# Where TensorE's operands start in SBUF: moving five tile pairs of a spectral MLP kernel to other offsets within 128 bytes

## The chip, the cores and the metric

The kernel runs on one core of a Trainium2 chip. The metric is the device time of one execution in microseconds. The reported time is the median of three runs. One further execution was recorded by the hardware profiler; every duration below comes from that one.

## The reference

The input `x` has 8 sequences of 3008 steps with 256 features. The reference takes a real FFT along the sequence, applies a complex 256 by 256 linear layer with bias to every frequency, soft-thresholds real and imaginary parts at 0.01, transforms back, and sends the 24064 resulting tokens through a two-layer MLP (256 to 2048 to 256) with a leaky ReLU:

```
X = rfft(x, axis=1);  Xr, Xi = X.real, X.imag
Yr = Xr @ w_r - Xi @ w_i + b_r
Yi = Xr @ w_i + Xi @ w_r + b_i
Yr, Yi = sign(Y) * max(abs(Y) - 0.01, 0)      # each of the two
y = irfft(Yr + 1j*Yi, n=3008, axis=1)          # 24064 tokens x 256
h = y @ moe_w_in;  g = max(0.01*h, h)
out = g @ moe_w_out
```

The MLP's weights arrive as float64 and are converted on the chip.

## The kernel before, in words

**Number format.** Nearly every product is made of float32 numbers that are split into a high and a low part in the format fp32r. A product is then three matmuls: high by high, high by low, low by high (`products`, L80, and `block`, L94, both helpers that record every product under one line). Each matmul needs a load of its 128 stationary columns, then streams 256 or 512 moving columns.

**Stages.** The FFT of length 3008 = 47 x 64 is done as small dense transforms. `fwd` (per sequence) folds and transforms over the 47: stationary `fa0`/`fa1`, moving `xz`, in PSUM tag psf. `mid` transforms over the 64 (`stage_b`, L358, plain float32, stationary `u`, moving `fb`), multiplies by the linear layer (`proj`: stationary `eh`, the transformed data; moving the 256-column weights `wr`, `wn`, `wd`), thresholds, and transforms back over the 64 (`stage_g`: stationary `gb`, moving `zh`, 512 columns). `inverse` (L495, plain float32) transforms back over the 47. `forms` makes the moving operands `yh`, `yl` of the MLP.

**The MLP.** Tokens go in 47 chunks of 512. The first layer (`moe_a`, `moe_b`, L94) uses seven products of 256 moving columns in place of eight: stationary `win_hi`/`win_lo`, moving `yh`/`yl`. Chunk 0 alone is done by `direct` with 512 moving columns. ScalarE and VectorE apply the leaky ReLU and split the result into `gh` and `gl` (`halves`, L573 and L575). The second layer (`moe_o`, L622) has stationary `wout_hi`/`wout_lo` and moving `gh`/`gl`, 512 columns.

**Order.** `moe` emits, for each of 8 steps of each chunk, the 21 matmuls of `moe_a`/`moe_b` and then 12 of `moe_o`, in the order in which they stand in the program. The work of `fwd`, `mid` and `inverse` for later sequences is fed between them by `Stream.to`, so that TensorE meets runs of one kind of matmul that are now and then broken by runs of another kind. A planner inside the tile framework sets the order of the rest from its own cost estimates; nothing in them depends on an operand's address.

**Places.** A tile is one stretch of bytes in each partition. The framework puts tiles one behind the other in steps of 32 bytes. `pair` allots constants with 32 floats to spare and starts them `skip` floats (4 bytes each) in. The list of tile addresses of the built program gives these starts, modulo 128 bytes:

| product | line | moving columns | matmuls | stationary starts at | moving starts at |
|---|---|---|---|---|---|
| first MLP layer, chunks 1 to 46 | L94 | 256 | 7728 | `win` 0 | `yh`,`yl` 64 |
| first MLP layer, chunk 0 | L94 | 512 | 96 | `win` 0 | `yh`,`yl` 64 |
| second MLP layer | L622 | 512 | 4512 | `wout` 64 | `gh`,`gl` 64 |
| linear layer (`proj`) | L80 | 256 | 1512 | `eh` 64 | `wr`,`wn`,`wd` 96 |
| `stage_g` | L80 | 512 | 252 | `gb` 64 | `zh` 64 |
| `stage_a` | L80 | 512 or 256 | 216 and 36 | `fa0`,`fa1` 64 | `xz` 64 |

Within one tile all slices that a matmul reads lie a multiple of 512 bytes apart, so every matmul of a row has the row's starts. The plain float32 matmuls (L358, L495 and those of the first sequences) are not in the table.

Of the kernel before, what the change touches and what calls it, by code (L numbers as in the profile page):

```python
# [9 lines left out]
F32R = mybir.dt.float32r  # L10
# [10 lines left out]
P = 128  # L21
PA = NK1 * NG
# [8 lines left out]
def spectral_mlp_kernel(  # L31
# [18 lines left out]
    D = w_r.shape[0]  # L50
    DF = w_in.shape[1]
    NF = DF // P
    NH = D // P
    NPAIR = NK1 // 2
    NQ = NF // 2
    NT, HT = 512, 256
# [9 lines left out]
    sb = ctx.enter_context(tc.tile_pool(name="sb", bufs=2))  # L66
# [4 lines left out]
    def bank(tag, bufs):  # L71
        return ps.tile([P, 512], F32, name=tag, tag=tag, bufs=bufs)
# [29 lines left out]
    def pair(name, shape, skip, spare=0):  # L102

        n = 1
        for s in shape[1:]:
            n *= s
        room = -(-n // 32) * 32 + 32
        tiles = [
            const.tile([shape[0], room + k], F32R, name=f"{name}_{p}")[:, skip:skip + n]
            for p, k in (("hi", 0), ("lo", spare))  # L110
        ]
        if len(shape) == 4:
            tiles = [t.rearrange("p (a b c) -> p a b c", a=shape[1], b=shape[2]) for t in tiles]
        elif len(shape) == 3:
            tiles = [t.rearrange("p (a b) -> p a b", a=shape[1]) for t in tiles]
        consts[name] = tuple(tiles)
        return consts[name]

    def load_plain(name, src, shape):
        consts[name] = const.tile(shape, F32, name=name)  # L120
        sync.dma_start(consts[name], src)

    def split_consts():
        for name in ("wr", "wd", "wn", "gb", "fa0", "fa1"):
            w = consts[name + "32"][0]
            hi, lo = pair(name, list(w.shape), 16 if name[0] == "w" else 8, 32 if name == "gb" else 0)
            act.copy(hi, w)
            dve.tensor_sub(lo, w, hi.bitcast(F32))

# [60 lines left out]
    def load_wout():  # L190

        n = CS // D
        ov = w_out.bitcast(U32).rearrange("(a p) f -> p a f", p=P)
        raws = []

        def load(early):
            k = len(raws)
            tag, bufs = ("gl", 2) if early else (("e", 1), ("z", 1))[k % 2]
            raw = sb.tile([P, CS, 2], U32, name="raw", tag=tag, bufs=bufs)
            with tc.issue_after(reads[13 if early else -1].ins):  # L200
                sync.dma_start(raw.rearrange("p (a f) w -> p a (f w)", a=n), ov[:, k * n:(k + 1) * n, :])
            raws.append(raw)

        for k in range(2):
            load(True)
        yield 1
        consts["wout"] = tuple(
            sb.tile([P, NF, D], F32R, name=f"wout_{p}", tag=f"wout_{p}", bufs=1) for p in ("hi", "lo"))
        for c in range(NF // n):
            a = sb.tile([P, CS], F32, name="cva", tag="zf", bufs=1)  # L210
            q = sb.tile([P, CS], F32, name="cvq", tag="u", bufs=3)
            float64_parts(raws[c], a, q)
            dh, dl = (w[:, c * n:(c + 1) * n, :] for w in consts["wout"])
            a, q = (t.rearrange("p (a f) -> p a f", a=n) for t in (a, q))
            act.copy(dh, a)
            dve.tensor_sub(a, a, dh.bitcast(F32))
            converted.append(dve.tensor_add(dl, a, q))
            yield 1
            while c >= 1 and len(raws) < min(c + 3, NF // n):
                load(False)  # L220
# [10 lines left out]
    def fwd(b):  # L231
        ud = dram.tile([2, NK1, NG * NS, D], F32, name="u_dram", tag="u_dram", bufs=NPRE + 1)
        u_dram[b] = ud
        uv = ud.rearrange("c k (g s) d -> c (k g) (s d)", g=NG)
        x_t, s_t = {}, {}

        def load(c):
            cols = slice(2 * c * D, min(2 * c + 2, NS) * D)
            n = cols.stop - cols.start
            if b < NPRE:  # L240
                tag, bufs = (XT, XT1)[b][c]
                x2 = sb.tile([PA, 2, 2 * D], F32, name="xin", tag=tag, bufs=bufs)
                x_t[c] = [x2[:, h, :n] for h in range(2)]
            else:
                x_t[c] = [
                    sb.tile([PA, 2 * D], F32, name=f"xin{h}", tag="uv"[h], bufs=3 - h)[:, :n] for h in range(2)
                ]
            for h, t in enumerate(x_t[c]):
                if b == 0:
                    (act if h else sync).dma_start(t, x[b, h, :, cols])  # L250
                else:
                    with tc.issue_after(reads[-1].ins):
                        sync.dma_start(t, x[b, h, :, cols])

        def fold(c):
            xa, xb = x_t[c]
            n = xa.shape[1]
            eng = dve
            xs = sb.tile([PA, 2 * D], F32, name="xs", tag="zf", bufs=1)[:, :n] if b else xs3[:, c % 3, :n]
            eng.tensor_add(xs, xa, xb)  # L260
            eng.tensor_sub(xa, xa, xb)
            s_t[c] = [(xs,), (xa,)] if b < NPRE else [xs, xa]

        def split(c, h):
            t = s_t[c][h]
            n = t.shape[1]
            z = sb.tile([PA, 2, 2 * D], F32R, name="xz", tag="ez"[h], bufs=1)
            xh, xl = z[:, 0, :n], z[:, 1, :n]
            dve.tensor_copy(xh, t)
            dve.tensor_sub(xl, t, xh.bitcast(F32))  # L270
            s_t[c][h] = (xh, xl)

        def stage_a(c, h):
            t = x_t[c][h]
            n = t.shape[1]
            pa = (bank("psf", 2) if b else bank("psh", 4))[:PA, :n]
            products(pa, [(consts[f"fa{h}"] if b else consts[f"fa{h}32"], s_t[c][h])])
            t = x_t[c][1 - h]
            cp = act.copy(t, pa)
            if b == 0:  # L280
                turned[:] = [cp]
            st = (act if b else sync).dma_start(uv[h, :, 2 * c * D:2 * c * D + n], t)
            if b == 0:
                written.append(st)

        def stage_a1(c):

            n = x_t[c][0].shape[1]
            pas = [(bank("psf", 2) if c in (4, 5) else bank("psh", 4))[:PA, :n] for _ in range(2)]
            for h in range(2):  # L290
                with tc.issue_after(turning[NPAIR - 2].ins):
                    products(pas[h], [
                        (consts[f"fa{h}32"], (x_t[c][0],)), (consts[f"fa{2 * h}32"], (x_t[c][1],))])
            for h in range(2):
                act.copy(x_t[c][h], pas[h])
                sync.dma_start(uv[h, :, 2 * c * D:2 * c * D + n], x_t[c][h])

        if b == 1:
            for c in range(NX):
                load(c)  # L300
                yield 0
            for c in (0, 1, 2, 3, 6, 4, 5):
                stage_a1(c)
                yield 6 * x_t[c][0].shape[1]
            return

        ahead = 2 if b >= NPRE else NX
        for c in range(ahead):
            load(c)
        yield 4 * CS if b >= NPRE else 0  # L310
        fold(0)
        if b >= NPRE:
            split(0, 0)
        yield 0
        for c in range(NX):
            for h in range(2):
                if h == 0 and c + ahead < NX:
                    load(c + ahead)
                if h == 0 and c + 1 < NX:
                    fold(c + 1)  # L320
                stage_a(c, h)
                if b >= NPRE and (c + h < NX):
                    split(c + h, 1 - h)
                yield 3 * x_t[c][h].shape[1]


    def mid(b):
# [21 lines left out]
        def stage_b(j):  # L349
# [4 lines left out]
            for i in range(2):  # L354
                k = 2 * j + i
# [4 lines left out]
            if b == 0:  # L360
# [2 lines left out]
                dve.tensor_add(ef[:, :, 2, :], ef[:, :, 0, :], ef[:, :, 1, :])  # L363
                e_t[j] = (ef,)
                return
            e2 = sb.tile([P, 2, NH, 3, P], F32R, name="eh", tag="e", bufs=1)
            eh, el = e2[:, 0], e2[:, 1]
            xi = sb.tile([P, NH, P], F32, name="xi", tag="xi", bufs=1)
            act.copy(xi, pv[:, :, 1, :])
# [7 lines left out]
        def proj(j):  # L377

            e = e_t.pop(j)
# [21 lines left out]
            t = sb.tile([P, 2, D], F32, name="t", tag="t" if b else "v", bufs=1 if b else 2)  # L401
# [12 lines left out]
            if b == 0:  # L414
                z_t[j] = (zf,)
                yield 6 * D
                return
            z = sb.tile([P, 2, 2, D], F32R, name="zh", tag="z", bufs=1)
            zh, zl = z[:, 0], z[:, 1]
            act.copy(zh, zf)  # L420
            dve.tensor_sub(zl, zf, zh.bitcast(F32))
# [147 lines left out]
        halves(ci, q, g)  # L569

    def halves(ci, q, g):
        gh = sb.tile([P, 4, HT], F32R, name="gh", tag="gh")
        cp = act.copy(gh, g)  # L573
        gl = sb.tile([P, 4, HT], F32R, name="gl", tag="gl")
        parted[:] = [cp, dve.tensor_sub(gl, g, gh.bitcast(F32))]  # L575
        g_t[ci, q] = (gh, gl)

# [154 lines left out]
    with tc.issue_after(reads[3].ins):  # L732
        load_plain("ga", ga, [PA, 2, P])
# [152 lines left out]
```

## Time and profile before

| what | value |
|---|---|
| median of 3 runs | 2558.36 us (2555.57 to 2559.72) |
| profiled execution, its own time | 2558.46 us |
| its span, first to last instruction | 2556.7 us |
| mean granted TensorE clock | 0.995 |
| TensorE matmuls busy | 2515.7 us (98%), 16204 records |
| TensorE weight loads busy | 2259.0 us (88%) |
| VectorE busy | 1881.0 us (74%) |
| ScalarE busy | 1673.5 us (65%) |
| GpSimd busy | 119.3 us (5%) |

Busy time of TensorE is a sum of durations that overlap: a matmul of 256 columns is shown as some 280 ns long while the next starts some 115 ns after it. What a matmul costs in a stream is therefore the distance from its start to the next start, which the timeline gives to 10 ns; over a run of matmuls the distance is exact enough to divide. The duration of one, given to the nanosecond, moves with that distance. A plain float32 matmul stands in the trace as two records.

### The profile page before, as it was taken

How to read it: one execution, taken by the hardware profiler on the slowest of the kernel's cores; microseconds unless marked ns; L12 is line 12 of the kernel's file. 1: busy time of each engine (PE TensorE's matmuls, PEld its weight loads, DVE VectorE, ACT ScalarE, POOL GpSimd, SP SyncE). 2: the span in 40 equal slices, each digit the busy share in tenths (PEclk: the TensorE clock that was granted, in tenths of full speed). 3: DMA queues.
4: the chain of work that ended last, by engine and by line, in shares of the span. 5: the costliest groups of instructions: out<-in, count | busy, mean ns of one | idle time of the engine just before them, and what ended most of it. 6: DMA issues, size and time to landing. Idle time of an engine off the chain costs nothing.

```text
span 2556.7 us, 42449 instructions
## 1 busy us (share of the span) xinstructions
PE 2515.7 (98%) x16204; PEld 2259.0 (88%) x16204; DVE 1881.0 (74%) x3460; ACT 1673.5 (65%) x3151; POOL 119.3 (5%) x96
## 2 busy tenths in 40 slices
PE   6999999999999999999999999999999999999999
PEld 4689888999899998999989999899998998999998
DVE  7787777777877778777787777876768777666675
ACT  4776666677666776667756676566665676656564
POOL 0001000000000000000000000000000000000000
PEclk8999999999999999999999999999999999999999
DMA  8631133111321113211142111411114111101000
GB/s 262 184 93 49 44 88 91 42 46 49 102 70 42 50 41 109 61 51 50 38 113 58 50 45 42 113 57 50 46 38 123 55 51 44 46 17 33 9 17 17
DMA packets 119904, 165.12 MB, mean 65 GB/s; under 512 B 13597, under 2 KB 69909, under 8 KB 119701
## 3 DMA queue, kind: packets, MB, share of 16 engines
q1 hardware_dynamic: 79112, 115.54, 14.9%
q10 hardware_dynamic: 40589, 46.87, 7.1%
q8 instruction: 128, 2.10, 0.3%
q14 instruction: 75, 0.61, 0.1%
HBM read 86.60 MB, written 75.76 MB: 64 GB/s over the span
## 4 chain that ended last, share of the span: by engine, by line
PE 90%; DMA 4%; DVE 3%; ACT 2%; issue 1%; SPq 1%; ACTq 0%; DVEq 0%
PE pso L622 38%; PE psh L94 34%; PE psf L80 11%; PE psf L495 3%; PE psf L358 3%; DMA xin<-x_dram 1%; PE psh L80 1%; DMA u<-u_dram 1%; DVE gl L575 1%; DMA u_dram<-xin 1%; DVE xz L270 0%; DMA v_dram<-v 0%; DVE gf L606 0%; ACT zf L413 0%; DMA vin<-v_dram 0%
## 5 line engine op out<-in xcount | busy, mean ns | idle before, releaser
L94 PE MATMUL psh<-yh,win_hi 128*128 128x256 f32 (+1 forms) x2608 | 737.2, 284 | 2.4 <-DVE gf L606 2.4
L94 PE MATMUL psh<-yl,win_hi 128*128 128x256 f32 (+1 forms) x2608 | 727.0, 279 | 0.0
L94 PE MATMUL psh<-yh,win_lo 128*128 128x256 f32 (+1 forms) x2608 | 726.5, 280 | 0.0
L575 DVE TENSOR_TENSOR gl<-gf,gh 128x1024 fp32r<-128x1024 f32 x376 | 461.1, 1226 | 309.7 <-ACT gh L573 300.5
L622 PE MATMUL pso<-gh,wout_hi 128*128 128x512 f32 x1504 | 592.3, 394 | 1.1 <-ACT gh L573 1.1
L622 PE MATMUL pso<-gh,wout_lo 128*128 128x512 f32 x1504 | 590.4, 393 | 0.0
L622 PE MATMUL pso<-gl,wout_hi 128*128 128x512 f32 x1504 | 588.7, 391 | 1.1 <-DVE gl L575 1.1
L94 PEld LDWEIGHTS psh<-yh,win_hi 128*128 128x128 f32 x2608 | 489.3, 188 | 19.9 <-DVE gf L606 4.9
L94 PEld LDWEIGHTS psh<-yl,win_hi 128*128 128x128 f32 x2608 | 490.5, 188 | 15.6 <-issue 0.5
L94 PEld LDWEIGHTS psh<-yh,win_lo 128*128 128x128 f32 x2608 | 489.1, 188 | 2.0
L573 ACT CAST gh<-gf 128x1024 fp32r<-128x1024 f32 x376 | 395.4, 1052 | 45.1 <-PE pso L622 35.3
L609 ACT ACTIVATE gf<-gf 128x768 f32<-128x768 f32 x368 | 311.8, 847 | 158.7 <-DVE gf L606 147.6
L622 PEld LDWEIGHTS pso<-gl,wout_hi 128*128 128x128 f32 x1504 | 282.6, 188 | 61.9 <-DVE gl L575 3.0
L622 PEld LDWEIGHTS pso<-gh,wout_hi 128*128 128x128 f32 x1504 | 282.7, 188 | 48.4 <-ACT gh L573 1.9
L622 PEld LDWEIGHTS pso<-gh,wout_lo 128*128 128x128 f32 x1504 | 282.6, 188 | 45.4 <-issue 0.2
L608 ACT ACTIVATE gf<-psh 128x256 f32<-128x256 f32 x368 | 141.6, 385 | 229.8 <-PE psh L94 223.4
L606 DVE TENSOR_TENSOR gf<-psh,u 128x512 f32<-128x512 f32 x368 | 252.7, 687 | 27.7 <-PE psh L94 25.3
L590 ACT COPY p<-psh 128x256 f32<-128x256 f32 x368 | 136.7, 371 | 153.3 <-PE psh L94 144.7
L395 POOL TENSOR_TENSOR kb<-bias,kc 128x512 f32<-128x512 f32 x84 | 116.7, 1389 | 2068.3 <-ACT kc L393 1865.4
L591 DVE TENSOR_TENSOR u<-psh,p 128x256 f32<-128x256 f32 x368 | 154.8, 421 | 71.8 <-ACT p L590 70.8
L593 DVE TENSOR_TENSOR gf<-psh,u 128x256 f32<-128x256 f32 x368 | 155.1, 422 | 30.4 <-PE psh L94 16.4
L594 DVE TENSOR_TENSOR gf<-psh,gf 128x256 f32<-128x256 f32 x368 | 154.8, 421 | 5.5
(128 smaller groups left out, 3179.4 us busy)
## 6 DMA issues: line engine op xcount, KB each, us to landing
u<-u_dram SPq DMA_DIRECT2D x192, 128.0 KB, 2.8
v_dram<-v ACTq DMA_DIRECT2D x192, 128.0 KB, 2.4
out_dram<-ob SPq DMA_DIRECT2D x94, 256.0 KB, 2.0
vin<-v_dram SPq DMA_DIRECT2D x96, 240.0 KB, 3.6
xin<-x_dram SPq DMA_DIRECT2D x90, 240.0 KB, 3.1
u_dram<-xin ACTq DMA_DIRECT2D x72, 240.0 KB, 2.4
u_dram<-xin SPq DMA_DIRECT2D x24, 240.0 KB, 4.3
raw<-w_out_dram SPq DMA_DIRECT2D x8, 512.0 KB, 4.9
```

The source lines that it names most:

```text
L80: last = nc.tensor.matmul(dst, a, b, start=(i == 0), stop=(i == len(terms) - 1))
L94: mlp[:] = [nc.tensor.matmul(dst, a, b, start=start and i == 0, stop=i == 2, skip_group_check=True)]
L573: cp = act.copy(gh, g)
L575: parted[:] = [cp, dve.tensor_sub(gl, g, gh.bitcast(F32))]
L590: act.copy(p1, b1[:, lo])
L591: dve.tensor_add(u2, b1[:, hi], p1)
L593: dve.tensor_add(g[:, 3], b2[:, hi], u2)
L594: dve.tensor_add(g[:, 3], b2[:, lo], g[:, 3])
L606: dve.tensor_add(g[:, 1:3], b2.rearrange("p (k n) -> p k n", k=2), u2.unsqueeze(1).broadcast_to([P, 2, HT]))
L608: act.activation(g[:, 0], b1[:, lo], AF.Prelu, alpha=SLOPE)
L609: act.activation(g[:, 1:4], g[:, 1:4], AF.Prelu, alpha=SLOPE)
L622: mlp[:] = [nc.tensor.matmul(po, a[:, f, s], r[:, i], start=(f == 0 and j == 0), stop=(f == NF - 1 and j == 2),)]
```

## The change

Every fp32r operand that TensorE reads is given a fixed start modulo 128 bytes: stationary ones 0, moving ones of 256 columns 64, moving ones of 512 columns 0. A new helper, `placed`, allots a tile with 128 bytes to spare and returns the part that begins 64 bytes in; `pair` gets other `skip` values. No instruction, tile count, buffer count or order in the program's text is altered; eight buffers grow by 128 bytes each, and every tile behind them moves up by a multiple of 128 bytes.

| product | stationary | moving |
|---|---|---|
| first MLP layer (L94), all chunks | 0, as before | 64, as before |
| second MLP layer (L622) | 64 to 0 | 64 to 0 |
| linear layer (L80, `proj`) | 64 to 0 | 96 to 64 |
| `stage_g` (L80) | 64 to 0 | 64 to 0 |
| `stage_a` (L80) | 64 to 0 | 64 to 0 |

```diff
+    def placed(shape, name, tag, bufs):
+        n = 1
+        for k in shape[1:]:
+            n *= k
+        t = sb.tile([P, n + 32], F32R, name=name, tag=tag, bufs=bufs)[:shape[0], 16:16 + n]
+        axes = " ".join("abcd"[:len(shape) - 1])
+        return t.rearrange(f"p ({axes}) -> p {axes}", **dict(zip("abcd", shape[1:])))
...
-            hi, lo = pair(name, list(w.shape), 16 if name[0] == "w" else 8, 32 if name == "gb" else 0)
+            hi, lo = pair(name, list(w.shape), 8 if name[0] == "w" else 24, 32 if name == "gb" else 0)
...
-            sb.tile([P, NF, D], F32R, name=f"wout_{p}", tag=f"wout_{p}", bufs=1) for p in ("hi", "lo"))
+            placed([P, NF, D], f"wout_{p}", f"wout_{p}", 1) for p in ("hi", "lo"))
...
-            z = sb.tile([PA, 2, 2 * D], F32R, name="xz", tag="ez"[h], bufs=1)
+            z = placed([PA, 2, 2 * D], "xz", "ez"[h], 1)
...
-            e2 = sb.tile([P, 2, NH, 3, P], F32R, name="eh", tag="e", bufs=1)
+            e2 = placed([P, 2, NH, 3, P], "eh", "e", 1)
...
-            z = sb.tile([P, 2, 2, D], F32R, name="zh", tag="z", bufs=1)
+            z = placed([P, 2, 2, D], "zh", "z", 1)
...
-        gh = sb.tile([P, 4, HT], F32R, name="gh", tag="gh")
+        gh = placed([P, 4, HT], "gh", "gh", 2)
...
-        gl = sb.tile([P, 4, HT], F32R, name="gl", tag="gl")
+        gl = placed([P, 4, HT], "gl", "gl", 2)
```

## The prediction

> **What bounds the kernel now.** I read the page's totals first, then what TensorE waited for, then TensorE's groups, then its timeline, since only that shows how far apart two matmuls start.
>
> ```profile
> span 2556.7 us, 42449 instructions
> PE 2515.7 (98%) x16204; PEld 2259.0 (88%) x16204; DVE 1881.0 (74%) x3460; ACT 1673.5 (65%) x3151; POOL 119.3 (5%) x96
> PEclk8999999999999999999999999999999999999999
> PE 90%; DMA 4%; DVE 3%; ACT 2%; issue 1%; SPq 1%; ACTq 0%; DVEq 0%
> ```
>
> TensorE holds 90% of the chain that ended last, at the full granted clock after the first slice. In the list of TensorE's own waits the longest two are single transfers of the first 100 us, and those on the MLP's data are tiny:
>
> ```profile
> PE psh L358 <- DMA u<-u_dram: 12.4, 2, 9.9
> PE psh L94 <- DVE gf L606: 2.4, 4, 1.0
> PE pso L622 <- DVE gl L575: 1.1, 2, 0.5
> ```
>
> VectorE and ScalarE have 26% and 35% of the span free. So a nanosecond saved or lost on each matmul moves the end by as much, and the case is decided by the distances between matmul starts. A clean step late in the run, 12 matmuls of L622 and then 21 of L94:
>
> ```profile
> 2314.06 0.40 PE L622 MATMUL pso<-gh,wout_hi 128*128 128x512 f32 x1
> ...
> 2315.44 0.39 PE L622 MATMUL pso<-gh,wout_hi 128*128 128x512 f32 x1
> ...
> 2316.80 0.28 PE L94 MATMUL psh<-yh,win_hi 128*128 128x256 f32 x1
> ...
> 2317.39 0.28 PE L94 MATMUL psh<-yh,win_lo 128*128 128x256 f32 x1
> ...
> 2319.20 0.40 PE L622 MATMUL pso<-gh,wout_hi 128*128 128x512 f32 x1
> ```
>
> The first six of L622 take 1.38 us (230 ns each), the last six 1.36 (226.7). The first five of L94 take 0.59 us (118 each), the other 16 take 1.81 (113.1). After a change of kind a run begins slowly and settles within about six matmuls, at 113 ns per 256 columns and 227 per 512. A run of the linear layer does not settle, and the L94 run behind one settles late:
>
> ```profile
> 1592.78 0.29 PE L80 MATMUL psf<-wn_hi,eh 128*128 128x256 f32 x1
> ...
> 1594.22 0.28 PE L94 MATMUL psh<-yh,win_hi 128*128 128x256 f32 x1
> ...
> 606.23 0.28 PE L94 MATMUL psh<-yh,win_hi 128*128 128x256 f32 x1
> ...
> 607.30 0.28 PE L94 MATMUL psh<-yh,win_hi 128*128 128x256 f32 x1
> ...
> 608.55 0.28 PE L94 MATMUL psh<-yh,win_lo 128*128 128x256 f32 x1
> ```
>
> Twelve products with `eh` take 1.44 us, 120 ns each. In the L94 run at 606.23, which follows such products, the first nine take 1.07 us (119 each) and the next eleven 1.25 (113.6). And in chunk 0, where L94 streams 512 columns from 64 against stationary operands at 0, twelve take 2.78 us, 231.7 each, with no settled end:
>
> ```profile
> 157.02 0.40 PE L94 MATMUL psh<-yh,win_hi 128*128 128x512 f32 x1
> ...
> 159.80 0.40 PE L622 MATMUL pso<-gh,wout_hi 128*128 128x512 f32 x1
> ```
>
> L622 has both its operands at 64 and settles. So with 256 columns the pair (stationary 0, moving 64) settles and (64, 96) does not; with 512 columns (64, 64) settles and (0, 64) does not. I read this as an effect of where the two operands lie **relative to each other**. Under that reading L622 keeps its distance of 0, and only the linear layer changes its own, from 32 to L94's 64.
>
> **The change part by part.** The medians by line (minimum, median, maximum in ns) give the size over the whole run; the duration of a settled 256-column matmul is 276.
>
> ```profile
> L94 PE MATMUL psh<-yh,win_hi x2608: 276/276/802, 122.0 to 2545.7; 128*128 128x256 f32 x184, 128*128 128x512 f32 x3
> L80 PE MATMUL psf<-wr_hi,eh x336: 277/282/385, 175.5 to 2186.0; 128*128 128x256 f32 x168
> L80 PE MATMUL psf<-wn_hi,eh x336: 278/280/288, 175.7 to 2189.5; 128*128 128x256 f32 x168
> L80 PE MATMUL psf<-wd_hi,eh x336: 277/281/363, 176.4 to 2190.2; 128*128 128x256 f32 x168
> L80 PE MATMUL psf<-wr_lo,eh x168: 277/281/286, 175.6 to 2185.9; 128*128 128x256 f32 x168
> L80 PE MATMUL psf<-wn_lo,eh x168: 277/281/286, 175.8 to 2189.3; 128*128 128x256 f32 x168
> L80 PE MATMUL psf<-wd_lo,eh x168: 277/281/365, 176.6 to 2190.0; 128*128 128x256 f32 x168
> ```
>
> *Linear layer (`wr`, `wn`, `wd` 96 to 64, `eh` 64 to 0).* Medians average 281, five above settled, over 3 x 336 + 3 x 168 = 1512 matmuls: 7.6 us. It becomes the same kind as L94, and a run that follows L94 should simply go on settled. In the timeline 109 of its runs follow L622; those should pay the slow start that L94 pays there, 5 x (118 - 113) = 25 ns at most where the run is long enough, some 20 ns: 2.2 us back. Gain 5.4 us. Bounds: 0 (the price stays) and 1512 x (120 - 113), 10.6.
>
> *L94 behind the linear layer.* 126 of its runs follow such products directly. The one quoted loses 9 x (119 - 113) = 54 ns; many are too short or settle sooner, and the mean over the 126, each start-to-start distance less 113.3, is 29 ns. If both are one kind nothing has to settle: 126 x 29 = 3.6 us. Bounds 0 and 126 x 54 = 6.8.
>
> *L622 (`wout`, `gh`, `gl` 64 to 0).* Relative place unchanged: I take 0, and keep wide bounds, since no row shows 512 columns with both operands at 0. Below: the slow start of the quoted step, 6 x (230 - 226.7) = 20 ns in 12 matmuls, is gone: 4512 / 12 x 20 = 7.5 us, and with the settled pace cut too it could be more. Above: the pace of chunk 0 everywhere, 231.7 against the step's 2.74 / 12 = 228.3, so 4512 x 3.4 = 15.3 us lost. I stay at 0 because the row nearest in kind is L622 itself.
>
> *`stage_g` and `stage_a`.* Same relative place, 504 matmuls in runs of a few: 0, with bounds of 504 x 3.4 = 1.7 us either way.
>
> The Trainium skill, page "TensorE: Matmul & The Clock Gate", section "Back-to-back issue gap", speaks against any effect: a warm gap is N / 2.4 + 2.5 ns, with the column count as its only variable. By it every 256-column matmul would cost 109.2 ns and every 512-column one 215.8 wherever it lies, and the sum would be nil. The trace disagrees: 113 and 120 for the same 256 columns.
>
> *The writers of the moved tiles.* They cost nothing if VectorE and ScalarE do not care for the start. `win_lo` and `win_hi` are written at 0, `gl` and `gh` at 64:
>
> ```profile
> L575 DVE TENSOR_TENSOR gl<-gf,gh 128x1024 fp32r<-128x1024 f32 x376 | 461.1, 1226 | 309.7 <-ACT gh L573 300.5
> L187 DVE TENSOR_TENSOR win_lo<-ws,win_hi 128x1024 fp32r<-128x1024 f32 x4 | 4.9, 1225 | 2.1 <-ACT win_hi L186 2.1
> L573 ACT CAST gh<-gf 128x1024 fp32r<-128x1024 f32 x376 | 395.4, 1052 | 45.1 <-PE pso L622 35.3
> L186 ACT CAST win_hi<-ws 128x1024 fp32r<-128x1024 f32 x4 | 4.2, 1046 | 3.2 <-DVE ws L183 3.2
> ```
>
> 1226 against 1225 and 1052 against 1046: nothing. Were a writer dearer, TensorE's small waits and the free quarter of VectorE would cover some tens of ns per tile. No transfer is issued, moved or resized, and no queue sees another order; the raw weights that share these buffers keep their starts.
>
> *What is late next.* Nine microseconds earlier on TensorE over the 46 chunks asks VectorE and ScalarE for 0.4% more pace, which their free shares cover.
>
> **Sum.** -5.4 - 3.6 + 0 = -9.0 us against the profiled execution's 2558.46 us (its span and 1.8 us around it), which stands 0.1 us above the median: 2549.4 us.
>
> **The rivals.**
> *Half gained, and L622 too (R1).* What counts is also the place itself: a stream from 0 touches fewer 128-byte stretches than one from 64, and with every stationary operand at 0 a change of kind disturbs less. For it: slow starts come just where L94 (stationary at 0) and L622 (at 64) alternate. Against: chunk 0's L94 and L622 differ in the same way, and the L94 run there settles nowhere. Price: 7.5 us of slow starts of L622, 5 x 5 = 25 ns for each of the 250 L94 runs that follow L622 directly in the timeline (6.2 us), on top of 9.0: -22.7, so 2536 us.
>
> *L622 never settles (R2, the other side).* What counts is the stationary operand: at 0 it is good for 256 columns and bad for 512, as chunk 0 has it. Then L622 takes chunk 0's pace: +15.3, `stage_g` and `stage_a` up to +1.7, the linear layer still -9.0: +8, 2566 us. It decides from 9.0 us / 4512 = 2.0 ns per matmul. Against: in chunk 0 the moving operand is at 64, not at 0.
>
> *Nothing happens (R3).* The linear layer's pace comes from its short runs and its operands' order, not from places; the rule cited above gives the same end. 2558.5 us. For it: it is never met in a run longer than 12. Against: L94 settles within six.
>
> **How the numbers follow.** My forecast 0.40, R1 0.25, R2 0.17, R3 0.18. This kernel's three runs lie 0.16% apart, so about 0.2% (5 us) can be told from no change. The forecast is faster by 0.35% with little of it inside the bound (0.03), R1 is faster, R3 the same, R2 slower by 0.3%: faster 0.62, same 0.21, slower 0.17. The range reaches down past R1 to 2530, for L622's settled pace may move by a nanosecond or two (4512 x 1.5 = 6.8 us), and up to R2, 2566. The forecast's own range is 2541 (its upper bounds, 10.6 + 6.8) to 2554.
>
> **What the profile after would show.** Right: the six rows of `eh` at medians of 276 to 277; a run of twelve of them behind L94 in 1.36 us; the L94 run behind them settled from its first matmul; L622 still at 1.38 and 1.36 us for its halves; L575 and L573 unchanged. R1 would show the first six of L622 in 1.36, or the last six below it. R2 would show twelve of L622 in 2.78. R3 would leave medians of 281. I would be wrong above all if 512 columns do not follow the relative place: each nanosecond there is worth 4.5 us, half my forecast.

## The result, and the profile after

The changed kernel is slower: 2583.49 us, the median of four runs (2578.24 to 2587.99), against 2558.82 for four runs of the kernel before (2555.57 to 2559.72). The ratio is 1.0095, its 95% interval 1.0081 to 1.0109. The forecast was 2549.4 and its range ended at 2566.

The profiled execution of the changed kernel took 2583.86 us at the same mean granted clock, 0.995. From its page, the span, the busy time of the engines and the shares of the chain that ended last:

```profile
span 2582.0 us, 42449 instructions
PE 2539.8 (98%) x16204; PEld 2274.3 (88%) x16204; DVE 1883.9 (73%) x3460; ACT 1676.7 (65%) x3151; POOL 118.4 (5%) x96
PE 93%; DMA 3%; DVE 2%; ACT 1%; issue 1%; SPq 0%; ACTq 0%; DVEq 0%
```

The instructions are as many as before, and the span is 25.3 us longer. TensorE holds three points more of the chain; VectorE and ScalarE changed by 3 us each. The writers of the moved tiles, in the page's costliest groups (busy us, mean ns of one, idle time before them and what ended it):

```profile
L584 DVE TENSOR_TENSOR gl<-gf,gh 128x1024 fp32r<-128x1024 f32 x376 | 461.1, 1226 | 311.1 <-ACT gh L582 307.8
L582 ACT CAST gh<-gf 128x1024 fp32r<-128x1024 f32 x376 | 394.6, 1050 | 45.6 <-PE pso L631 37.6
```

They take 1226 and 1050 ns, where they took 1226 and 1052. So the loss lies in the distances between matmul starts. A clean step of the same kind as the one in the prediction, from the timeline (start, duration; L631 is the old L622):

```profile
2340.36 0.39 PE L631 MATMUL pso<-gh,wout_hi 128*128 128x512 f32 x1
...
2341.74 0.40 PE L631 MATMUL pso<-gh,wout_hi 128*128 128x512 f32 x1
...
2343.14 0.28 PE L94 MATMUL psh<-yh,win_hi 128*128 128x256 f32 x1
...
2343.73 0.28 PE L94 MATMUL psh<-yh,win_lo 128*128 128x256 f32 x1
...
2345.61 0.39 PE L631 MATMUL pso<-gh,wout_hi 128*128 128x512 f32 x1
```

Neither run settles now. L631's halves take 1.38 and 1.40 us (before 1.38 and 1.36). L94's first five take 0.59 us as before, but its other 16 take 1.88, 117.5 ns each where they took 113.1. The rows by line and tile (minimum, median, maximum in ns) show it over the whole run:

```profile
L94 PE MATMUL psh<-yh,win_hi x2608: 275/282/801, 121.6 to 2571.0; 128*128 128x256 f32 x184, 128*128 128x512 f32 x3
L94 PE MATMUL psh<-yl,win_hi x2608: 275/281/398, 122.1 to 2571.1; 128*128 128x256 f32 x184, 128*128 128x512 f32 x3
L631 PE MATMUL pso<-gh,wout_lo x1504: 387/395/628, 133.7 to 2577.5; 128*128 128x512 f32 x188
L631 PE MATMUL pso<-gl,wout_hi x1504: 387/393/628, 133.9 to 2577.7; 128*128 128x512 f32 x188
L80 PE MATMUL psf<-wr_hi,eh x336: 276/280/388, 175.4 to 2205.0; 128*128 128x256 f32 x168
L80 PE MATMUL psf<-wr_lo,eh x168: 275/281/283, 175.5 to 2204.8; 128*128 128x256 f32 x168
```

The same view of the kernel before, for one row of the first layer and two of the second that the prediction did not show:

```profile
L94 PE MATMUL psh<-yl,win_hi x2608: 275/276/397, 122.5 to 2545.8; 128*128 128x256 f32 x184, 128*128 128x512 f32 x3
L622 PE MATMUL pso<-gh,wout_lo x1504: 387/393/484, 134.1 to 2552.1; 128*128 128x512 f32 x188
L622 PE MATMUL pso<-gl,wout_hi x1504: 387/389/499, 134.3 to 2552.3; 128*128 128x512 f32 x188
```

L94's medians in these rows went from 276 to 281 and 282 (a settled matmul is 276, a slow one 281). L622's went from 393 and 389 to 395 and 393. The linear layer, whose six medians were to fall to 276 or 277, stands at 279 to 281, at most two below before.

To add this up I took every distance from one matmul's start to the next in the timeline, less the settled pace (113.3 ns for 256 columns, 226.5 for 512), and summed over all runs of matmuls of a kind. The 1.5% of distances that hold a longer stall are left out; any cut between 25 and 80 ns above the pace gives the same sums within 0.2 us. I call this the **excess**; all excesses below are worked out so.

| excess, us | L94 | L622 | linear layer | sum of the three |
|---|---|---|---|---|
| before | 14.5 | 13.7 | 9.2 | 37.4 |
| after | 32.4 | 23.4 | 6.7 | 62.5 |
| difference | +17.9 | +9.7 | -2.5 | +25.1 |

The sum accounts for 25.1 of the 25.3 us by which the span grew. Some seven tenths of the loss is in L94, of which the change's table said "as before".

**What moved.** The starts given ahead of the prediction are modulo 128 bytes. The list of tile addresses, taken modulo 256, shows more:

| operands | before, modulo 256 | after, modulo 256 |
|---|---|---|
| `win_hi`, `win_lo` | 128, 0 | 128, 0 |
| `yh`, `yl` | 64, 64 | **192**, 64 |
| `wout_hi`, `wout_lo` | 64, 64 | **128, 0** |
| `gh`, `gl` | 64, 64 | **128 or 0**, by buffer |
| `eh`; weights `_hi`, `_lo` | 64; 96, 224 | 0; 64, 192 |

The pads of 128 bytes put `yh` 640 bytes further, 128 modulo 256, against `yl` and `win`. The second layer's four operands, all in step before, are now at two places.

### The profile page after: what moved, and what is told of

It reads as the page before. It is cut to its first block, busy times and chain, and to the rows that moved or that the text cites. A ratio compares the mean times of both kernels' runs of the same rounds, so it can differ in the third digit from the quotient of the medians.

```text
span 2582.0 us, 42449 instructions
## 1 busy us (share of the span) xinstructions
PE 2539.8 (98%) x16204; PEld 2274.3 (88%) x16204; DVE 1883.9 (73%) x3460; ACT 1676.7 (65%) x3151; POOL 118.4 (5%) x96
## 3 DMA queue, kind: packets, MB, share of 16 engines
q1 hardware_dynamic: 79112, 115.54, 14.6%
## 4 chain that ended last, share of the span: by engine, by line
PE 93%; DMA 3%; DVE 2%; ACT 1%; issue 1%; SPq 0%; ACTq 0%; DVEq 0%
PE pso L631 39%; PE psh L94 35%; PE psf L80 11%; PE psf L504 3%; PE psf L367 3%; DMA xin<-x_dram 1%; PE psh L80 1%; DMA u<-u_dram 1%; DMA win_raw<-w_in_dram 0%; PE psh L367 0%; DVE gl L584 0%; DMA vin<-v_dram 0%; ACT zf L422 0%; DVE gf L615 0%; DMA u_dram<-xin 0%
## 5 line engine op out<-in xcount | busy, mean ns | idle before, releaser
L94 PE MATMUL psh<-yh,win_hi 128*128 128x256 f32 (+1 forms) x2608 | 743.5, 286 | 1.6 <-DVE gf L615 1.6
L94 PE MATMUL psh<-yl,win_hi 128*128 128x256 f32 (+1 forms) x2608 | 734.9, 282 | 0.0
L94 PE MATMUL psh<-yh,win_lo 128*128 128x256 f32 (+1 forms) x2608 | 730.4, 281 | 0.0
L584 DVE TENSOR_TENSOR gl<-gf,gh 128x1024 fp32r<-128x1024 f32 x376 | 461.1, 1226 | 311.1 <-ACT gh L582 307.8
L631 PE MATMUL pso<-gh,wout_hi 128*128 128x512 f32 x1504 | 594.8, 395 | 1.0 <-ACT gh L582 1.0
L631 PE MATMUL pso<-gh,wout_lo 128*128 128x512 f32 x1504 | 594.9, 396 | 0.0
L631 PE MATMUL pso<-gl,wout_hi 128*128 128x512 f32 x1504 | 593.5, 395 | 1.3 <-DVE gl L584 1.3
L94 PEld LDWEIGHTS psh<-yh,win_hi 128*128 128x128 f32 x2608 | 490.4, 188 | 20.3 <-DVE gf L615 4.3
L94 PEld LDWEIGHTS psh<-yl,win_hi 128*128 128x128 f32 x2608 | 490.3, 188 | 16.7 <-issue 0.5
L94 PEld LDWEIGHTS psh<-yh,win_lo 128*128 128x128 f32 x2608 | 489.9, 188 | 2.0
L582 ACT CAST gh<-gf 128x1024 fp32r<-128x1024 f32 x376 | 394.6, 1050 | 45.6 <-PE pso L631 37.6
L631 PEld LDWEIGHTS pso<-gl,wout_hi 128*128 128x128 f32 x1504 | 283.5, 188 | 64.2 <-DVE gl L584 2.8
L631 PEld LDWEIGHTS pso<-gh,wout_hi 128*128 128x128 f32 x1504 | 283.3, 188 | 49.4 <-ACT gh L582 1.8
L631 PEld LDWEIGHTS pso<-gh,wout_lo 128*128 128x128 f32 x1504 | 283.1, 188 | 48.0 <-issue 0.2
```

Source lines behind the costliest of these rows:

```text
L94: mlp[:] = [nc.tensor.matmul(dst, a, b, start=start and i == 0, stop=i == 2, skip_group_check=True)]
L631: mlp[:] = [nc.tensor.matmul(po, a[:, f, s], r[:, i], start=(f == 0 and j == 0), stop=(f == NF - 1 and j == 2),)]
```

## The experiments

In the diffs `gap(name, n)` allots an unused tile of n bytes, which moves what is allotted behind it; a second gap, where there is one, brings the rest back into place modulo 256. In `e4_second64`, `f3_wout64`, `g1_rule256`, `g3_woutlo128` and `h1_after_yh` work tiles of the other engines move along, and in `f2_proj64` one of the two `xz`. The diffs are cut to their core. Unless another base is named, each is an edit of the kernel before. Several are single runs: fifteen runs of the kernel before lie 8.8 us apart (2555.46 to 2564.22), so a difference of that size between two single runs says nothing, and there the rows decide.

**Is it `yh`, and with which period?** Three single runs move `yh` by 128, by 256, and `yh` and `yl` together by 128. A fourth puts the whole second layer at 0 modulo 128 while keeping it in step. The kernel before took 2559.36 beside them.

`e1_yh128`

```diff
+    gap("gap_yh", 128)
...
+    gap("gap_yh_end", 384)
```

> The kernel before, with 128 spare bytes ahead of yh and 384 behind it: yh alone moves, by 128 bytes, everything else keeps its place modulo 512. Modulo 128 nothing changes. Theory A (places count beyond 128 bytes; the change lost its time because the 128-byte pads moved yh by 640 bytes against yl and win): L94 no longer settles at 113 ns but stays near 118, and the time rises by about 7728 x 2.3 = 18 us, to some 2576. Theory B (only the place modulo 128 counts, as the prediction had it, and L94's loss came from its new neighbours): L94 settles at 113, 2558 us.

`e2_yh256`

```diff
+    gap("gap_yh", 256)
...
+    gap("gap_yh_end", 256)
```

> The same with yh alone moved by 256 bytes. Theory A with a period of 256 bytes: L94 settles at 113 again, 2558 us. Theory A with a period of 512 bytes or more: L94 stays slow, 2570 to 2580 us. Theory B: 2558 us, whatever the first run shows.

`e3_both128`

```diff
+    gap("gap_yl", 128)
...
+    gap("gap_yl_end", 384)
...
+    gap("gap_yh", 128)
...
+    gap("gap_yh_end", 384)
```

> yh and yl both moved by 128 bytes, so that they agree with each other modulo 512 but lie otherwise against win. Theory A1 (the two moving operands must agree with each other): L94 settles at 113, 2558 us. Theory A2 (the distance between moving and stationary operands counts, beyond 128 bytes): L94 stays slow, near 2576 us. Theory B: 2558 us.

Measured: 2573.92, 2560.78 and 2573.84 us. The row of `yl` on `win_hi` of the three, in this order, one fence for each:

```profile
L94 PE MATMUL psh<-yl,win_hi x2608: 275/281/397, 120.9 to 2561.2; 128*128 128x256 f32 x184, 128*128 128x512 f32 x3
```

```profile
L94 PE MATMUL psh<-yl,win_hi x2608: 275/277/415, 121.4 to 2548.1; 128*128 128x256 f32 x184, 128*128 128x512 f32 x3
```

```profile
L94 PE MATMUL psh<-yl,win_hi x2608: 275/281/415, 122.3 to 2561.1; 128*128 128x256 f32 x184, 128*128 128x512 f32 x3
```

`yh` alone by 128 bytes costs 14.6 us and raises L94's excess from 14.5 to 32.3, the changed kernel's 32.4. By 256 bytes it costs nothing (median 277, excess 14.3). So for `yh` **the period is 256 bytes, not 128**. With `yl` moved along, L94 stays slow in the sum (excess 31.8): that the two moving operands agree is not enough, their distance to `win` counts.

The sum hides one thing in this third run. Most of the L94 runs directly behind the plain float32 matmuls of `stage_b` (L358, here L361) do settle, while those behind the second layer and the linear layer go at 118. One run behind `stage_b`, its second matmul and the one after its last:

```profile
1190.04 0.28 PE L94 MATMUL psh<-yl,win_hi 128*128 128x256 f32 x1
...
1192.31 0.39 PE L625 MATMUL pso<-gh,wout_hi 128*128 128x512 f32 x1
```

Twenty matmuls take 2.27 us, 113.5 each: with one and the same set of places a run can go at either pace, by what ran before it.

`e4_second64`

```diff
+                gap("gap_wout_lo", 64)
...
+                    gap("gap_gl", 64)
...
+    gap("gap_yh", 448)
```

> gl, gh, wout_hi and wout_lo all moved by 64 bytes, so that the second layer has both operands at 0 modulo 128 as in the change, but all four still agree modulo 512; yh, yl, win, eh, zh keep their places modulo 512 (vin, yc and some work tiles move by 64 too). Theory A (agreement counts, not the place itself): L622 as before, first six 230 ns, then 226.7, 2558 us. Theory C (512 columns lose at 0 modulo 128): L622 near 231.5 throughout as in the changed kernel, about 4512 x 2.2 = 10 us more, 2568 us.

Measured: 2557.67 us. `gl`, `gh`, `wout_hi` and `wout_lo` all start at 128 modulo 256, which is 0 modulo 128, the place the change wanted. One row:

```profile
L629 PE MATMUL pso<-gh,wout_lo x1504: 387/389/628, 131.1 to 2551.3; 128*128 128x512 f32 x188
```

The median is 389 (before 393), the excess 10.9 (before 13.7): L622 even settles sooner. A start at 0 modulo 128 is harmless in itself; what the changed kernel's second layer lacks is the common place. L94, none of whose operands moved, went from 14.5 to 18.8, more than half of it in the runs directly behind the moved L622, which settle later.

**What is the relation?** Four single runs beside 2555.76 for the kernel before: `yl` alone moved, so that L94's moving operands differ the other way; the linear layer as the change wanted it, but in step modulo 256; `wout` against `gh`/`gl` by 64; and L94's four operands all at one place, as L622 has them.

`f1_yl128`

```diff
+    gap("gap_yl", 128)
...
+    gap("gap_yl_end", 128)
```

> The kernel before with yl alone moved by 128 bytes (to 192 modulo 256; yh stays at 64, win_hi at 128, win_lo at 0). Theory D (signed distance: while a matmul streams, the next one's stationary operand is loaded; 256 columns run undisturbed where that load starts 64 above the moving operand modulo 256, and suffer where it starts 64 below): all three distances of L94 become +64, so L94 settles at 113 ns at least as early as before, 2550 to 2558 us. Theory E (absolute place: a moving operand of 256 columns must start at 64 modulo 256): a third of L94's matmuls is disturbed, at least 6 us more, 2565 us or above. Theory A1 (yh and yl must agree): 2574 us, as when yh alone moved.

Measured: 2583.95 us, the worst for L94, excess 46.7. I had not expected it of this distance. Its row:

```profile
L94 PE MATMUL psh<-yl,win_hi x2608: 276/284/399, 119.5 to 2571.2; 128*128 128x256 f32 x184, 128*128 128x512 f32 x3
```

The stationary load that runs beside a matmul is the next one's: in the kernel before, `yh` on `win_hi` starts at 2317.84 us and the load for the next matmul, `yl` on `win_hi`, at 2317.85. In L94's order (`yh` on `win_hi`, `yl` on `win_hi`, `yh` on `win_lo`) the loads stand, against the operand streaming meanwhile, at +64, -64, +64 bytes in the kernel before. Moving `yl` turns this into three times +64 and still the run does not settle (112 to 130 ns, wandering): the distances alone are not the rule. `g4_winlo128` below has the same three distances with both moving operands at one place, and its runs hold a steady 118 or 113. So the 128 bytes between the moving operands may be what makes this run worse; but `yl` changed its place against the tile that it multiplies, too, and no run separates the two.

`f2_proj64`

```diff
-        room = -(-n // 32) * 32 + 32
+        room = -(-n // 32) * 32 + (64 if name in ("wr", "wd", "wn") else 32)
...
-            hi, lo = pair(name, list(w.shape), 16 if name[0] == "w" else 8, 32 if name == "gb" else 0)
+            hi, lo = pair(name, list(w.shape), 8 if name[0] == "w" else 8, 32 if name == "gb" else 0)
...
+            gap("gap_e", 64)
...
+            gap("gap_e_end", 192)
```

> The kernel before with the linear layer alone moved: wr, wn, wd high and low all at 64 modulo 256 (128 more spare bytes in each of the six tiles), eh at 128, every load 64 above its moving operand; the rest keeps its place modulo 256. Theory D: the linear layer settles at 113 ns (medians of 276 to 277 in its six groups instead of 281), L94 settled behind it, 6 to 9 us less, some 2550 us: the prediction's step with the right period. Rival (the linear layer's runs of up to 12 are too short to settle): medians near 281 remain, 2558 us.

Measured: 2549.57 us, 6.2 below the one run of the kernel before beside it; its span, 2547.8, is 8.9 below the profiled one of the kernel before. Rows of the linear layer, then a run of twelve behind L94 and one behind L622 (now L627), first matmul and the one after the last:

```profile
L80 PE MATMUL psf<-wr_hi,eh x336: 276/276/386, 173.9 to 2177.2; 128*128 128x256 f32 x168
L80 PE MATMUL psf<-wn_hi,eh x336: 276/281/283, 174.2 to 2180.6; 128*128 128x256 f32 x168
L80 PE MATMUL psf<-wd_hi,eh x336: 276/277/367, 174.8 to 2181.3; 128*128 128x256 f32 x168
```

```profile
1586.97 0.28 PE L80 MATMUL psf<-wn_hi,eh 128*128 128x256 f32 x1
...
1588.33 0.28 PE L94 MATMUL psh<-yh,win_hi 128*128 128x256 f32 x1
...
1682.25 0.28 PE L80 MATMUL psf<-wr_hi,eh 128*128 128x256 f32 x1
...
1683.66 0.28 PE L94 MATMUL psh<-yh,win_hi 128*128 128x256 f32 x1
```

Twelve behind L94 take 1.36 us, 113.3 each, exactly what the prediction wanted to see. The run behind L622 stays at 118 (1.41 us for twelve) and never settles. Four of the six medians are at 276 or 277; those of `wn` stay at 281 and 280. Excess of the linear layer 9.2 to 3.0, of L94 14.5 to 11.3: the two terms of the prediction, got by the same idea with the right period.

`f3_wout64`

```diff
+            gap(f"gap_{tag}", (64, 64)[c // 2])
...
+    gap("gap_wout_hi_end", 192)
```

> The kernel before with wout_hi and wout_lo alone moved by 64 bytes, to 128 modulo 256 (gh, gl stay at 64): every load of L622 starts 64 above its moving operand. Theory D with 512 columns like 256: L622 settles at 227 or sooner than before, 2550 to 2558 us. Theory D with 512 columns wanting distance 0: L622 never settles, near 231.5 as in chunk 0, 10 to 15 us more, 2570 us.

Measured: 2573.06 us. A run of twelve in its timeline:

```profile
2332.22 0.39 PE L626 MATMUL pso<-gh,wout_hi 128*128 128x512 f32 x1
...
2335.01 0.28 PE L94 MATMUL psh<-yh,win_hi 128*128 128x256 f32 x1
```

2.79 us, 232.5 each, with no settled end (excess 28.2). With 512 columns loads at 0 from the stream settle and loads at +64, where two of L94's three stand, do not: L622's excess grows by 14.5 us.

`f4_first0`

```diff
-        room = -(-n // 32) * 32 + 32
+        room = -(-n // 32) * 32 + (64 if name == "win" else 32)
...
+    gap("gap_yl", 64)
...
+    gap("gap_yl_end", 192)
...
+    gap("gap_yh", 64)
...
+    gap("gap_yh_end", 192)
```

> The kernel before with yh, yl, win_hi and win_lo all at 128 modulo 256: every load of L94 starts at its moving operand's place, distance 0. Theory D (256 columns want +64): L94 does not settle, 117 to 119 ns, 2574 us or above. Rival (what counts is only that all loads of a run have the same distance, as in L622, whichever it is): L94 settles at 113, 2558 us or less.

Measured: 2585.85 us.

```profile
L94 PE MATMUL psh<-yl,win_hi x2608: 274/283/398, 122.5 to 2573.1; 128*128 128x256 f32 x184, 128*128 128x512 f32 x3
```

All of L94 at one place, distance 0, does not settle with 256 columns: near 120 ns throughout, excess 45.9. The two column counts want different places. (The four stand at 128 here, where no other run has a stream of L94 or of the linear layer, so that the place itself has a part in this can't be ruled out.)

**The rule kept, the period mended; and the rest of the relation.** Beside these the kernel before took 2559.08 (median of ten, 2556.2 to 2562.6).

`g1_rule256` keeps the change's starts modulo 128 and puts each pair in step modulo 256; its core:

```diff
+        if name != "win":
+            room, spare = -(-n // 64) * 64 + (64 if name[0] != "w" else 0), 0
...
+                    gap("gap_gl", 64)
...
+            gap("gap_e", 64)
...
+    gap("gap_yh", 192)
```

> The change's own rule modulo 128 (stationary 0, moving 64 or 0), but with every operand pair kept in step modulo 256: yh, yl 64 and win 128/0 as in the kernel before; gh, gl, wout all 128; wr, wn, wd all 64 with eh at 128; zh, xz, gb, fa all 128. If the change lost its time only by the 128-byte steps of its pads (theory A, period 256): L94 settles at 113, L622 at 226.7, the linear layer at 113 behind L94 as in the run that moved it alone (6 us less); 2548 to 2555 us, faster than both kernels. If something in the rule modulo 128 itself costs time: 2560 us or more.

Measured: 2550.59 us, median of six (2548.05 to 2553.41); ratio 0.9968, 95% interval 0.9956 to 0.998.

```profile
L94 PE MATMUL psh<-yh,win_hi x2608: 276/276/802, 119.2 to 2535.2; 128*128 128x256 f32 x184, 128*128 128x512 f32 x3
L632 PE MATMUL pso<-gh,wout_lo x1504: 387/389/628, 131.3 to 2541.7; 128*128 128x512 f32 x188
```

276 and 389 again. Excess 16.3 (L94), 9.1 (L622) and 3.6 (linear layer). The same places modulo 128 that cost 25 us in the changed kernel gain 8.5 here.

`g2_all128`

```diff
+        room = -(-n // 32) * 32 + (32 if name != "win" else 96)
...
+    gap("gap_yl", 128)
...
+    gap("gap_yl_end", 128)
...
+    pair("win", [P, 7, NQ, P], 56)
...
+    gap("gap_yh", 128)
...
+    gap("gap_yh_end", 128)
```

> The kernel before with yh, yl, win_hi and win_lo all moved by 128 bytes: the distances of L94 are those of the kernel before, every absolute place modulo 256 is another. Distance theory (moving against stationary, modulo 256): L94 settles at 113, 2558 us, although yh and yl stand where they cost 15 us while win stayed. Absolute theory (a moving operand of 256 columns must start at 64 modulo 256): L94 near 118, 2574 us.

Measured: 2549.2 us, one run. All four operands of L94 moved by 128, and L94 keeps its settled pace and its excess (14.5): for the pace within a run of one kind it is the places relative to each other that count. Not expected by me: the gain of 9.9 us, from 2559.08. L622's excess fell from 13.7 to 6.4, and the median distances of its runs behind L94 go 226, 227, 227 from the first matmul where they went 232, 236, 228, 233. So the slow start of L622 behind L94 depends on where L94's operands lie against its own.

`g3_woutlo128`

```diff
+                gap("gap_wout_lo", 128)
```

> The kernel before with wout_lo alone moved by 128 bytes (to 192 modulo 256; wout_hi, gh, gl stay at 64): high and low stationary operands of L622 lie 128 apart, as in the changed kernel. Theory A: L622 no longer settles at 226.7 ns but stays near 231 as after the change, 8 to 12 us more, some 2567 us; L94 as before. Rival (L622's loss comes from starting at 0 modulo 128 or from its new neighbours): L622 settles, 2558 us.

`g4_winlo128`

```diff
+        room = -(-n // 32) * 32 + (64 if name == "win" else 32)
```

> The kernel before with win_lo alone moved by 128 bytes, to where win_hi lies modulo 256, so that every load of L94 starts 64 above its moving operand (before: two of three above, one below). If in-step operands are always best: L94 settles at 113 at least as early, 2550 to 2558 us. From the run that gave the linear layer this pattern (behind L94 it went on at 113, behind L622 it stayed at 118 for its twelve): the L94 runs that follow L622, 250 of them with 3050 matmuls, stay near 118 and the others vary, 10 to 25 us more, 2570 to 2580 us.

Measured: 2569.95 and 2570.17 us, one run each. One row of each kernel:

```profile
L627 PE MATMUL pso<-gh,wout_hi x1504: 387/396/795, 133.3 to 2563.4; 128*128 128x512 f32 x188
```

```profile
L94 PE MATMUL psh<-yl,win_hi x2608: 276/281/398, 121.8 to 2557.5; 128*128 128x256 f32 x184, 128*128 128x512 f32 x3
```

One tile of the second layer, `wout_lo`, 128 bytes away from its partner gives L622 an excess of 23.8; the changed kernel has 23.4, with the two `wout` 128 apart and the `g` buffers as well (no run has the `g` buffers alone so). `win_lo` in step with `win_hi` raises L94 to 26.8: 118 ns throughout behind L622, though behind the linear layer it settles at 113.

**How much of the loss is `yh`, and what is the best version?** The kernel before beside these: 2559.78, median of fifteen.

`h1_after_yh` is the changed kernel with `yh` put back in step:

```diff
-        t = sb.tile([P, n + 32], F32R, name=name, tag=tag, bufs=bufs)[:shape[0], 16:16 + n]
+        t = sb.tile([P, n + (16 if name == "wout_lo" else 32)], F32R, name=name, tag=tag, bufs=bufs)[:shape[0], 16:16 + n]
...
+    gap("gap_yh", 128)
...
+    gap("gap_yh_end", 128)
```

> The changed kernel with yh alone put back to 64 modulo 256 (128 spare bytes ahead of it and 128 behind; wout_lo's tile 64 bytes shorter at its end to make room); all other operands stay where the change put them modulo 256. If the loss is the sum of two displacements, yh's and L622's: L94 settles at 113 again and gives back the 18 us that moving yh alone cost it in the kernel before, L622 stays near 231: 2566 us. If the change's loss has another cause inside the changed kernel: L94 stays near 118, 2580 us or above.

Measured: 2565.56 us, median of ten (2563.21 to 2569.38); ratio to the kernel before 1.0024, 95% interval 1.0015 to 1.0033.

```profile
L94 PE MATMUL psh<-yl,win_hi x2608: 276/276/397, 122.0 to 2551.7; 128*128 128x256 f32 x184, 128*128 128x512 f32 x3
L634 PE MATMUL pso<-gh,wout_lo x1504: 387/395/484, 133.6 to 2558.1; 128*128 128x512 f32 x188
```

L94 settles again (excess 14.5) while L622 stays at 395 (excess 24.8). About 18 of the 25 us are `yh`'s 128 bytes; the rest is the second layer, whose excess is 11.1 above the kernel before's, less the 3.4 that the linear layer gains (9.2 to 5.8).

`h2_best` is `g2_all128` with the linear layer in step (weights 192, `eh` 0, so that every load stands 64 above its stream) and `gb` and `fa`, high and low, all at 64; its core beside that of `g2_all128`:

```diff
+        room = -(-n // 64) * 64
+        if name == "win":
+            room, spare = n + 96, 0
...
+            hi, lo = pair(name, list(w.shape), 0)
+            gap("gap_e", 192)
...
+            gap("gap_e_end", 64)
```

> Two gains together, on the kernel before: yh, yl at 192, win_hi at 0, win_lo at 128 (L94's distances as before, but its streams 128 away from L622's, as in the run where all four moved), and the linear layer at wr, wn, wd 192 with eh at 0 (every load 64 above), gb and fa high and low in step with zh at 64. If slow starts depend on where the streams of neighbouring runs lie against each other, and settled paces on the distances within a run, both gains add: about -10 and -6, some 2543 us. If the gain of moving all four came from its neighbours' places by accident: near 2550 us.

Measured: 2541.6 us, median of five (2540.25 to 2543.02); ratio 0.9932, 95% interval 0.9918 to 0.9946. It beats both kernels. From its page, the span and the busy times:

```profile
span 2538.5 us, 42449 instructions
PE 2498.5 (98%) x16204; PEld 2252.0 (89%) x16204; DVE 1880.1 (74%) x3460; ACT 1676.1 (66%) x3151; POOL 119.4 (5%) x96
```

Its row for L622 (now L631), and its clean step in the timeline:

```profile
L631 PE MATMUL pso<-gh,wout_lo x1504: 388/389/632, 131.8 to 2533.9; 128*128 128x512 f32 x188
```

```profile
2312.56 0.39 PE L631 MATMUL pso<-gh,wout_hi 128*128 128x512 f32 x1
...
2315.28 0.28 PE L94 MATMUL psh<-yh,win_hi 128*128 128x256 f32 x1
...
2317.67 0.39 PE L631 MATMUL pso<-gh,wout_hi 128*128 128x512 f32 x1
```

Twelve of L622 take 2.72 us, 226.7 each, settled from the first (before 2.74, after 2.78). The excesses are 12.3 (L94), 3.7 (L622) and 3.8 (linear layer), together 17.6 us under the kernel before; measured 18.2. It is the same instructions in the same order: only addresses differ.

## Why the prediction was wrong, point by point

- **A nanosecond on each matmul "moves the end by as much"**: right. The excess summed to 25.1 us and the span grew by 25.3; in `h2_best` 17.6 and 18.2.
- **"Relative to each other"**: right as an idea, wrong in its period. The prediction compared starts modulo 128, the only figures that its table held. `e1_yh128` and `e2_yh256` show 256.
- **"Under that reading L622 keeps its distance of 0, and only the linear layer changes its own"** is the step that failed. The same pads that carry the change push "every tile behind them", in the change's words, by multiples of 128, and the prediction gave that no term at all. Odd multiples change the place modulo 256: `yh` went to 192, which cost 17.9 us in L94, whose own runs had no term in the sum; `wout_hi`, `wout_lo` and the `g` buffers came to lie 128 apart, and L622 lost 9.7 where the prediction took 0. Its outer bound for L622, 15.3, held, but the bound for L94 was missing, and so the range ended too low.
- **Linear layer, -5.4**: -2.5 came (excess 9.2 to 6.7), for the `_hi` and `_lo` weights stayed 128 bytes apart. With the right period `f2_proj64` took 6.2 off this excess. **L94 behind it, -3.6**: lost in L94's general slowness; 3.2 came off L94's excess in `f2_proj64`. Both terms were sized well for a change that this was not.
- **R1 (the place itself, stretches of 128 bytes)** falls: `e4_second64` puts L622 at 0 modulo 128 without the 7.5 us that R1 took for its slow starts (2.8 less excess), and `g2_all128` gets 7.3 of them without touching L622's places. L94's excess, which R1 wanted 6.2 us lower, is 4.3 higher in `e4_second64`.
- **R2 (512 columns from a stationary operand at 0 never settle)** had the right sign and place, and the wrong mechanism: `e4_second64` has such operands and a median of 389. The changed L622 does not settle because its operands lie 128 apart: `g3_woutlo128` gets the same from one tile, and `g1_rule256` settles with all of them at 128.
- **R3 (places do nothing)** falls by 44 us between `h2_best` and `f4_first0`, which differ in nothing but addresses. The rule behind it (the Trainium skill, "TensorE: Matmul & The Clock Gate", "Back-to-back issue gap") makes the gap depend on the column count alone, but the section gives it for an isolated matmul and says that in a stream of load and matmul pairs both set the spacing; so it speaks less against an effect of places than the prediction took it to. 256 columns cost 113.3 to 120 ns here, by place.
- **Writers, transfers, other engines at nothing**: right (1226 and 1050 ns; VectorE's and ScalarE's busy times within 3.2 us of before, GpSimd's within 0.9).
- **Three details that decided nothing**: of the "longest two" waits only the longest, 9.9 us, is on a transfer; the next, 7.0 us, is on VectorE's `xs` (L260). The linear layer is met in runs longer than 12, of 13, 16 and 18, and they do not settle either, which was one more point against R3. The forecast's own range "to 2554" does not come out of its lower bounds of 0, which give 2558.

What stays open is why. The runs give the pattern below and no cause: no counter of the trace shows what a stream and a load have in common.

## What to carry to other kernels

Where a stream of matmuls is the bound, write down the starts of every stationary and moving operand modulo 256 bytes, before and after any edit that changes a tile's size, for the tiles that the edit names and for all that lie behind them. Judge it by the distance between starts: a run that settles within some nine matmuls of a change of kind has its places right, one that stays some 4 to 8 ns above the settled pace does not, or came behind a kind that does not suit it. An unused tile of 64 or 128 bytes is a cheap trial; in this kernel moving tiles by such steps was worth 0.7%.

## What the runs showed of the hardware

- The place of TensorE's fp32r operands modulo 256 bytes moves the pace of a stream, at granted clocks of 0.994 to 0.996: 113.3 against 117 to 122 ns for 256 columns, 226.7 against 231 to 236 for 512. Duration medians go from 276 to 281 and more, and from 389 to 395.
- The reading that fits the runs best is that it counts where the next stationary operand, which is loaded meanwhile, lies from the operand that streams. In the order of the three matmuls of a product:

| columns | loads against the stream, bytes | where | pace, ns |
|---|---|---|---|
| 256 | +64, -64, +64 | L94 before, all moved by 128, `yh` by 256 | settles at 113 |
| 256 | -64, -64, -64 | L94 in the changed kernel, `e1_yh128` | 118, never settles |
| 256 | -64, +64, -64 | L94 in `e3_both128` | 118; mostly 113 behind `stage_b` |
| 256 | +64, +64, +64 | L94 in `g4_winlo128`, linear layer in `f2_proj64` | 118 behind L622; 113 behind the other of the two |
| 256 | +64, +64, +64, `yl` 128 from `yh` | L94 in `f1_yl128` | 112 to 130, wandering |
| 256 | 0, 0, 0 | L94 in `f4_first0` | 120 |
| 512 | 0, 0, 0 | L622 before, `e4_second64`, `h2_best` | settles at 227 |
| 512 | +64, +64, +64 | L622 in `f3_wout64` | 231 to 236 |
| 512 | 0 and 128 mixed | L622 in `g3_woutlo128`, the changed kernel | 229 to 237 |

- That the place of a load alters the pace of the stream beside it does not follow from the Trainium skill ("TensorE: Matmul & The Clock Gate", "Step-by-step: what each phase is for"), by which the two have read ports of their own and a load takes no bandwidth from a running matmul. Of TensorE's fp32r operands `g3_woutlo128` moves only a stationary tile, and it costs 10.9 us. Whether read bandwidth is what is lost, no run shows.
- A pace has a memory. The same products with equal distances run at 113 behind one kind of matmul and at 118 for the whole run behind another (`f2_proj64`: twelve in 1.36 us behind L94, 1.41 behind L622; `g4_winlo128` and `e3_both128` the same for L94). The slow starts between kinds go away when the neighbours' places suit, worth some 7 us of L622's excess in `g2_all128`. Which places suit for such a change of kind was not settled.
